# Running the last 64 rows of a 448-row contraction for two output blocks at once, in the two halves of the PE array

## The chip, the cores and the metric

The kernel runs on one core of a Trainium2 chip. The engines are named as in the profiles: PE (TensorE, the matmuls; PEld are its weight loads), ACT (ScalarE), DVE (VectorE), POOL (GpSimdE) and SP, whose queue issues most DMA transfers. PE writes its results to PSUM, a memory which the kernel divides into eight banks; ACT and DVE empty them (an "eviction"). The metric is the device time of one execution in microseconds (us), lower is better. Each version is timed several times beside the kernel before on the same chip.

The kernel before spreads from 334.6 to 340.4 us. Its shorter runs (up to 337 us) have a mean granted clock of 0.969 to 0.980 in the run records and its longer ones (from 338 us) of 0.955 to 0.965; the granted clock is the share of full speed that PE was allowed. A run over 1.5% above the fastest of its kernel counts as slow and is left out, and in some rounds that takes away a few of the longest runs of the kernel before. Differences under 1% are therefore read from intervals and from matmul spacings in the traces, not from single times.

## The reference

Two layers, each a spectral mixing half and a feed-forward half (FFN), over 2048 tokens of width D = 448:

```python
def _B_ref(x, w1, b1, w2, b2):            # the FFN; F = 1792
    h = jnp.einsum("bsd,df->bsf", x, w1) + b1
    r = jnp.where(h > 0, h, 0)
    h = r * r
    return jnp.einsum("bsf,fd->bsd", h, w2) + b2

# _A_ref: irfft2(rfft2(x) * W), computed in the kernel by matmuls with matrices of the Fourier transform
x = x + _A_ref(_layernorm(x), A_w_r, A_w_i)
x = x + _B_ref(_layernorm(x), B_w1, B_b1, B_w2, B_b2)
x = x + _A_ref(_layernorm(x), A_w_r, A_w_i)
x = x + _B_ref(_layernorm(x), B_w1, B_b1, B_w2, B_b2)
```

## The kernel before

The contraction of the first FFN matmul has 448 = 3 x 128 + 64 rows. The kernel before pads the last 64 rows with zero weights to a fourth block of 128. It works in four chunks c of 512 tokens; in each, `h_part` makes 14 blocks of h (128 features x 512 tokens) with 56 matmuls (a "W1 group"), and then four o tiles of 14 matmuls each use them (a "W2 group"). A "slot" below is the time from the start of one matmul to the start of the next.

```python
memset(W1_sb[64:128, 3, :], 0.0)
dma("sp", W1_sb[0:64, 3, :], B_w1[384:448, :])
...
def h_part(c, fb):
    hb = hbuf[c % 2]
    q = _Tile(1)                                  # one PSUM bank
    for blk in range(4):
        mm(q[lambda b: ps[:, b, :]], W1_sb[:, blk, fb * P:(fb + 1) * P], yT[:, 4 * c:4 * c + 4, blk, :],
           blk == 0, blk == 3)
    act(hb[:, fb, :], q[...], ACT.Relu, bias=b1f[:, fb:fb + 1])     # ScalarE empties the bank
    tt(hb[:, fb, :], hb[:, fb, :], hb[:, fb, :], ALU.mult)          # VectorE squares
...
def ffn(last):
    for t in range(0, NT, 2):
        sch.bias = 5500.0 * (NT - t)
        stage_TI(t); stage_AI(t)                  # inverse transforms of two token tiles
        ln_B1(t); ln_B2(t)                        # layer norm, transpose by DMA into yT
    for c in range(4):
        sch.bias = 22000.0 * (4 - c)
        for fb in range(FB):
            h_part(c, fb)
        for t in range(4 * c, 4 * c + 4):
            sch.bias = 5500.0 * (NT - t)
            o_tile(t)
            ...
```

The program's order is not written by hand. Every operation goes to a list scheduler that runs in Python when the kernel is built. It works with modelled costs, and takes next the unit that could start earliest, with ties broken by priority (`prio`, which includes `sch.bias`). All matmuls of one PSUM tile form one unit. The scheduler also picks each tile's PSUM banks, the ones free earliest by its own account:

```python
def pick_banks(n):
    best = None
    for b in range(0, NB, n):
        ok = [bank_user[i] is None or all(op in done for op in bank_user[i].readers) for i in range(b, b + n)]
        if all(ok):
            f = max(bank_free[b:b + n])
            if best is None or f < best[0]:
                best = (f, b)
    return best
...
key = (start, -u.prio, u.seq)
...
for a in (op.gdeps if e != "pe" else ()):         # the account of banks
    if a.eng == "pe" and a.unit.tile is not None:
        for i in range(a.unit.tile.bank, a.unit.tile.bank + a.unit.tile.n):
            bank_free[i] = max(bank_free[i], t + op.lat)
```

So an edit to one tile can change the order of the whole program.

## Time and profile before

| | |
|---|---|
| time | 338.5 us (338.15 to 339.89, 3 runs) |
| span in the profile | 336.8 us |
| PE / DVE / ACT busy | 85% / 61% / 53% |
| one W1 matmul, start to start | 216 ns (duration 379 ns) |

The first lines of the page of the kernel before: span, busy time and share per engine, and further down the shares of the chain that ended last.

```profile
span 336.8 us, 4428 instructions
...
PE 285.0 (85%) x1574; PEld 154.8 (46%) x1574; DVE 205.1 (61%) x499; ACT 178.5 (53%) x293; POOL 56.3 (17%) x81
...
PE 64%; DVE 24%; ACT 5%; issue 2%; POOL 2%; DMA 1%; DVEq 0%; POOLq 0%; ACTq 0%
```

The timeline of PE in the kernel before, second FFN. Columns: start and length in us, engine, source line, operation, output<-inputs, array rows x columns, shape, count; in brackets the idle time just before and what ended it.

```profile
235.60 1.47 PE L454 MATMUL ps<-TI_sb,VT 128*128 128x224 bf16 x8
...
241.90 13.95 PE L454 MATMUL ps<-yT,W_sb 128*128 128x512 bf16 x56 [1.96 <-ACT arena L472]
255.69 10.76 PE L454 MATMUL ps<-W_sb,arena 128*128 128x448 bf16 x56
266.28 12.25 PE L454 MATMUL ps<-yT,W_sb 128*128 128x512 bf16 x56
278.37 10.76 PE L454 MATMUL ps<-W_sb,arena 128*128 128x448 bf16 x56
288.96 10.52 PE L454 MATMUL ps<-yT,W_sb 128*128 128x512 bf16 x48
299.32 0.92 PE L454 MATMUL ps<-XA,FI_sb 128*128 128x448 bf16 x4
300.07 10.76 PE L454 MATMUL ps<-W_sb,arena 128*128 128x448 bf16 x56
310.67 12.25 PE L454 MATMUL ps<-yT,W_sb 128*128 128x512 bf16 x56
322.75 10.76 PE L454 MATMUL ps<-W_sb,arena 128*128 128x448 bf16 x56
```

`yT,W_sb` is the first FFN matmul (W1), `W_sb,arena` the second (W2). From 241.9 us to the end PE never waits. (The W1 group at 241.90 takes 13.95 and not 12.25 us, because seven of its first slots took 427 ns, at a lowered clock.)

### The profile page before, as it was taken

How to read it: one execution, taken by the hardware profiler on the slowest of the kernel's cores; microseconds unless marked ns; L12 is line 12 of the kernel's file. 1: busy time of each engine (PE TensorE's matmuls, PEld its weight loads, DVE VectorE, ACT ScalarE, POOL GpSimd, SP SyncE). 2: the span in 40 equal slices, each digit the busy share in tenths (PEclk: the TensorE clock that was granted, in tenths of full speed). 3: DMA queues.
4: the chain of work that ended last, by engine and by line, in shares of the span. 5: the costliest groups of instructions: out<-in, count | busy, mean ns of one | idle time of the engine just before them, and what ended most of it. 6: DMA issues, size and time to landing. Idle time of an engine off the chain costs nothing.

```text
span 336.8 us, 4428 instructions
## 1 busy us (share of the span) xinstructions
PE 285.0 (85%) x1574; PEld 154.8 (46%) x1574; DVE 205.1 (61%) x499; ACT 178.5 (53%) x293; POOL 56.3 (17%) x81
## 2 busy tenths in 40 slices
PE   0979857857799999899996975774799999999996
PEld 0656534533354454455454652443344445445442
DVE  5705992799867555776455499159973342463432
ACT  2669955655634706645813885555573271451730
POOL 4991000454300000200000000045530000010000
PEclk9999977999999999999999898799789999999999
DMA  7994000033210000010000000002231100002001
GB/s 300 409 371 75 1 2 0 0 69 70 50 34 0 0 2 0 0 34 1 0 2 0 0 2 0 0 0 65 63 79 31 41 0 29 27 0 74 14 14 41
DMA packets 25621, 16.00 MB, mean 48 GB/s; under 512 B 19392, under 2 KB 24000, under 8 KB 25600
## 3 DMA queue, kind: packets, MB, share of 16 engines
q1 hardware_dynamic: 25312, 15.43, 15.0%
q10 hardware_dynamic: 288, 0.30, 0.3%
q8 instruction: 12, 0.20, 0.2%
q14 instruction: 9, 0.07, 0.1%
HBM read 9.70 MB, written 1.84 MB: 34 GB/s over the span
## 4 chain that ended last, share of the span: by engine, by line
PE 64%; DVE 24%; ACT 5%; issue 2%; POOL 2%; DMA 1%; DVEq 0%; POOLq 0%; ACTq 0%
PE ps L454 64%; DVE tmp L476 7%; DVE x_sb L476 4%; DVE st L548 4%; DVE arena L476 3%; DVE tmp L485 2%; ACT arena L472 2%; DVE nmr L559 2%; ACT XA L472 2%; DMA x_sb<-in_A_x_dram 1%; ACT VT L472 1%; POOL Fs L485 1%; DVE mv L549 1%; POOL Ms L485 1%; DVE rstd L556 0%
## 5 line engine op out<-in xcount | busy, mean ns | idle before, releaser
L454 PE MATMUL ps<-yT,W_sb 128*128 128x512 bf16 x448 | 101.7, 387 | 5.6 <-ACT arena L472 5.6
L472 ACT ACTIVATE arena<-ps,b1f 128x512 bf16<-128x512 f32 x112 | 75.3, 685 | 47.0 <-PE ps L454 47.0
L454 PE MATMUL ps<-W_sb,arena 128*128 128x448 bf16 x448 | 86.9, 352 | 0.0
L476 DVE TENSOR_TENSOR arena<-arena 128x512 bf16<-128x512 bf16 x112 | 49.6, 443 | 40.0 <-ACT arena L472 39.9
L454 PEld LDWEIGHTS ps<-yT,W_sb 128*128 128x128 bf16 x448 | 44.2, 99 | 61.2 <-ACT arena L472 8.1
L476 POOL TENSOR_TENSOR arena<-x_sb,b2row 128x896 bf16<-128x896 bf16 x16 | 30.3, 1907 | 215.7 <-DVE x_sb L476 179.5
L454 PEld LDWEIGHTS ps<-W_sb,arena 128*128 128x128 bf16 x448 | 43.8, 98 | 40.1
L472 ACT ACTIVATE XA<-ps 128x512 bf16<-128x512 f32 (+1 forms) x48 | 32.5, 701 | 28.1 <-PE ps L454 27.7
L476 DVE TENSOR_TENSOR x_sb<-ps,arena 128x448 bf16<-128x448 f32 x32 | 19.9, 623 | 37.0 <-PE ps L454 37.0
L548 DVE BATCH_NORM_STATS2 st<-x_sb 128x6 f32<-128x448 bf16 x64 | 38.4, 614 | 3.0 <-DMA x_sb<-in_A_x_dram 2.4
L454 PE MATMUL ps<-H_sb,arena 128*128 128x256 bf16 x128 | 22.9, 330 | 11.3 <-DVE arena L476 9.9
L472 ACT ACTIVATE arena<-ps 128x904 bf16<-128x904 f32 x32 | 28.0, 931 | 5.9 <-PE ps L454 5.6
L472 ACT ACTIVATE rstd<-mv,epst 128x2 f32<-128x2 f32 (+1 forms) x40 | 11.7, 293 | 35.5 <-DVE mv L549 35.4
L476 DVE TENSOR_TENSOR x_sb<-ps,x_sb 128x896 bf16<-128x896 f32 x16 | 16.8, 1071 | 18.6 <-PE ps L454 18.6
L472 ACT ACTIVATE VT<-ps 128x512 bf16<-128x512 f32 (+1 forms) x36 | 18.6, 551 | 13.9 <-PE ps L454 13.6
L454 PEld LDWEIGHTS ps<-H_sb,arena 128*128 128x128 bf16 x128 | 13.5, 115 | 20.5 <-DVE arena L476 14.3
L454 PE MATMUL ps<-XA,FI_sb 128*128 128x448 bf16 x64 | 14.1, 354 | 9.5 <-ACT XA L472 9.5
L485 DVE TENSOR_SCALAR tmp<-x_sb,mv,rstd 128x224 bf16<-128x224 bf16 (+1 forms) x48 | 20.3, 453 | 1.4
L472 ACT ACTIVATE tmp<-x_sb,nmr,rstd 128x448 bf16<-128x448 bf16 x16 | 12.2, 759 | 13.1 <-DVE nmr L559 12.9
L476 DVE TENSOR_TENSOR tmp<-arena 128x904 bf16<-128x904 bf16 (+1 forms) x16 | 8.9, 567 | 16.2 <-ACT arena L472 16.1
L454 PE MATMUL ps<-Fs,x_sb 128*128 128x256 bf16 x32 | 9.8, 324 | 10.0 <-POOL Fs L485 9.1
L454 PE MATMUL ps<-arena,G_sb 128*128 128x452 bf16 (+1 forms) x72 | 15.1, 342 | 3.3 <-ACT arena L472 2.0
(40 smaller groups left out, 208.3 us busy)
## 6 DMA issues: line engine op xcount, KB each, us to landing
x_sb<-in_A_x_dram SPq DMA_DIRECT2D x4, 448.0 KB, 5.3
out_dram<-x_sb SPq DMA_DIRECT2D x16, 112.0 KB, 1.7
W_sb<-in_B_w_dram SPq DMA_DIRECT2D x1, 1568.0 KB, 19.7
W_sb<-in_B_w_dram SPq DMA_DIRECT2D x1, 1344.0 KB, 15.1
yT<-in_A_w_r_dram SPq DMA_DIRECT2D x1, 900.0 KB, 9.1
yT<-in_A_w_i_dram SPq DMA_DIRECT2D x1, 900.0 KB, 10.9
H_sb<-c_H SPq DMA_DIRECT2D x1, 896.0 KB, 12.1
G_sb<-c_G SPq DMA_DIRECT2D x1, 672.0 KB, 7.4
```

Source lines behind the costliest of these rows:

```text
L454: sch.add("pe", lambda e: e.matmul(_res(o), lhsT, rhs, start=start, stop=stop, skip_group_check=skip), [lhsT, rhs], [o], cost=max(_free(rh ...
L472: sch.add("act", lambda e: e.activation(o, _res(i), func, **kw), rd, [o], cost=c)
L476: sch.add(eng, lambda e: e.tensor_tensor(o, _res(a), b, op), [a, b], [o], cost=_free(o) / rate + 65.0)
L485: sch.add(eng, lambda e: e.tensor_scalar(o, i, s1, s2, op0=op0, **kw), rd, [o], cost=_free(o) / (1.4 if eng == "pool" else 1.92) + 65.0)
L548: small(lambda e, t=t: e.bn_stats(st[:, t, 0:6], x_sb[:, t, :]), [x_sb[:, t, :]], [st[:, t, 0:6]], 530.0)
L549: small(lambda e, t=t: e.bn_aggr(mv[:, t, 0:2], st[:, t, 0:6]), [st[:, t, 0:6]], [mv[:, t, 0:2]])
L559: small(lambda e: e.scalar_tensor_tensor(out=n, in0=m, scalar=-1.0, in1=r, op0=ALU.mult, op1=ALU.mult), [m, r], [n])
```

## The change

Two neighbouring blocks of h become one unit with a tile of two banks. Each block's first three matmuls stay. The fourth matmuls, now of 64 rows each, use the lower and the upper half of the array, so that they should stream at the same time. `yT` held the 64 rows twice already.

```diff
-        memset(W1_sb[64:128, 3, :], 0.0)
...
-        dma("sp", W1_sb[0:64, 3, :], B_w1[384:448, :])
+        for i in range(2):
+            dma("sp", W1_sb[64 * i:64 * i + 64, 3, :], B_w1[384:448, :])
...
         def h_part(c, fb):
             hb = hbuf[c % 2]
-            q = _Tile(1)
-            for blk in range(4):
-                mm(q[...], W1_sb[:, blk, fb * P:(fb + 1) * P], yT[:, 4 * c:4 * c + 4, blk, :], blk == 0, blk == 3)
-            act(...); tt(...)
+            q = _Tile(2)
+            yt = yT[:, 4 * c:4 * c + 4]
+            for i in range(2):
+                for blk in range(3):
+                    mm(q[lambda b, i=i: ps[:, b + i, :]], W1_sb[:, blk, (fb + i) * P:(fb + i + 1) * P],
+                       yt[:, :, blk, :], blk == 0, False)
+            for i in range(2):
+                r = slice(64 * i, 64 * i + 64)
+                mm(q[lambda b, i=i: ps[:, b + i, :]], W1_sb[r, 3, (fb + i) * P:(fb + i + 1) * P],
+                   yt[r, :, 3, :], False, True)
+            for i in range(2):
+                act(...); tt(...)                 # as before, per block
...
-                for fb in range(FB):
+                for fb in range(0, FB, 2):
                     h_part(c, fb)
```

The intent is to save one of eight 216 ns slots per pair of blocks.

More of the change, by code (lines that the diff above doesn't have):

```diff
@@ L725, in h_part @@
             hb = hbuf[c % 2]
-            q = _Tile(1)
-            for blk in range(4):
-                mm(q[lambda b: ps[:, b, :]], W1_sb[:, blk, fb * P:(fb + 1) * P], yT[:, 4 * c:4 * c + 4, blk, :],
-                   blk == 0, blk == 3)
-            act(hb[:, fb, :], q[lambda b: ps[:, b, :]], ACT.Relu, bias=b1f[:, fb:fb + 1])
-            tt(hb[:, fb, :], hb[:, fb, :], hb[:, fb, :], ALU.mult)
+            q = _Tile(2)
+            yt = yT[:, 4 * c:4 * c + 4]
+            for i in range(2):
+                for blk in range(3):
+                    mm(q[lambda b, i=i: ps[:, b + i, :]], W1_sb[:, blk, (fb + i) * P:(fb + i + 1) * P], yt[:, :, blk, :],
+                       blk == 0, False)
+            for i in range(2):
+                r = slice(64 * i, 64 * i + 64)
+                mm(q[lambda b, i=i: ps[:, b + i, :]], W1_sb[r, 3, (fb + i) * P:(fb + i + 1) * P], yt[r, :, 3, :],
+                   False, True)
+            for i in range(2):
+                act(hb[:, fb + i, :], q[lambda b, i=i: ps[:, b + i, :]], ACT.Relu, bias=b1f[:, fb + i:fb + i + 1])
+                tt(hb[:, fb + i, :], hb[:, fb + i, :], hb[:, fb + i, :], ALU.mult)
         def o_tile(t):
```

## The prediction

> **What bounds the kernel now.** The page gives a span of 336.8 us with PE busy 85%, DVE 61%, ACT 53%; the chain of waits is 64% PE. In it two long stretches hang on PE almost alone: 90.2 to 179.8 us and 241.9 to 333.5 us, the two FFN halves. The spectral stages are not touched. In the stretches PE's timeline has 56 W1 matmuls (128x512) in 12.25 us and 56 W2 matmuls in 10.76 us without a gap: one W1 matmul costs 216 ns start to start (its listed 379 ns is latency, with a tail of 163 ns that the next one covers). ACT (685 ns per block) and DVE (443 ns) keep up with PE's 864 ns per block. Before 90.2 and 241.9 PE waits for ACT, which stands behind the layer norm on DVE. The granted clock is 1.00, but for the first few us of the second FFN, where it was halved.
>
> **Removed.** A pair of blocks issues eight matmuls before and after, but the last two, of 64 rows each, should stream together in the two halves of the array: one 216 ns slot less per pair, 56 pairs, 12.1 us of PE. The Trainium skill, "TensorE: Matmul & The Clock Gate", Part 3, says that row tiles run concurrently, starting about 4 ns apart; no run shows it yet. 7 pairs (48 W1 matmuls of the first half lie before 90.2, 8 of the second before 241.9) run while PE waits for others anyway; 49 pairs count: 10.6 us at most.
>
> **Added.** One more 224 KB load, early: nothing. PSUM is taken two banks at a time and a pair's evictions come together: under 1 us. The real cost: each pair goes from 128-row to 64-row mode and back, 112 switches. "TensorEngine Tiling (Array Packing)", Key Properties, says that changing the tiling mode drains the TensorE; it gives no time, and the trace before has only 128-row matmuls, so nothing here measures it. Bounds from the trace: weights loaded with nothing ahead delay a matmul by some 10 ns (227 instead of 216 ns at 90.2 us); a full drain would show about the 163 ns tail. A free switch gains 10.6 us, 108 ns per switch nothing, 170 ns loses 6 us. My guess is 70 to 80 ns: 216 - 150 = 66 ns gained per pair, 49 pairs, about 3.3 us.
>
> **Prediction: 335 us**, 8 in 10 between 328 and 344. Faster by over 2%: 0.28; within 2%: 0.60; slower by over 2%: 0.12.
>
> **What would show the steps.** (1) The two 64-row matmuls of a pair start within 10 ns of each other. (2) The first of them starts later than 216 ns after the last full one, or the next full one later than 216 ns after the pair: the excess is the drain, 40 to 110 ns each. (3) A chunk of 56 W1 matmuls takes 11.3 to 12 us instead of 12.25. (4) W2 groups stay at 10.76 us, the spectral stages unchanged; PE stays the chain in both stretches.
>
> **What would make it wrong.** A switch that drains the whole tail, with weight loads that can't be pulled ahead across it (slower); a drain hidden or very short (up to 3% faster); row tiles that don't overlap (no gain and all the cost); a greedy schedule that turns out differently with two-bank tiles, above all in the first chunk, where PE waits for ACT.

## More of the kernel before

Look at the line at 299.32: four small matmuls of the *inverse transform* (the last token pair, t = 14) stand just ahead of the third W2 group. They are the second step of that transform; the first, eight matmuls `TI_sb,VT`, was done at 235.60, ahead of the whole FFN, and ACT carries its result to the second. Their result goes through the layer norm and a DMA transpose into `yT`, which the last W1 group (310.67) needs. All of that happens while PE works off the W2 group at 300.07, so nobody waits for it.

## The result, and the profile after

The changed kernel takes 349.2 us (349.18 to 351.81, 4 runs) against 338.32 us (338.03 to 339.89, 4 runs). Ratios here and below are the mean time of one kernel's fast runs over that of the other's of the same rounds, so they are not quite the ratio of the medians quoted. This one is 1.033 (95% interval 1.027 to 1.039): slower, and outside the predicted range.

The same lines of the page after:

```profile
span 347.4 us, 4466 instructions
...
PE 282.4 (81%) x1574; PEld 142.9 (41%) x1574; DVE 207.1 (60%) x498; ACT 173.2 (50%) x293; POOL 56.5 (16%) x81
...
PE 59%; DVE 27%; ACT 7%; issue 3%; DMA 2%; POOL 2%; POOLq 0%; DVEq 0%; ACTq 0%; SPq 0%
```

PE is *less* busy than before (282.4 against 285.0 us). What was added is time in which PE stands still. The timeline of PE after, second FFN, shows where:

```profile
249.56 5.22 PE L454 MATMUL ps<-yT,W_sb 128*128 128x512 bf16 x24 [1.54 <-ACT arena L472]
254.72 10.77 PE L454 MATMUL ps<-W_sb,arena 128*128 128x448 bf16 x56
265.33 12.12 PE L454 MATMUL ps<-yT,W_sb 128*128 128x512 bf16 x56
277.38 10.77 PE L454 MATMUL ps<-W_sb,arena 128*128 128x448 bf16 x56
287.98 10.40 PE L454 MATMUL ps<-yT,W_sb 128*128 128x512 bf16 x48
298.31 0.94 PE L454 MATMUL ps<-TI_sb,VT 128*128 128x224 bf16 x8
300.55 10.77 PE L454 MATMUL ps<-W_sb,arena 128*128 128x448 bf16 x56 [1.30 <-ACT XA L472]
311.15 0.92 PE L454 MATMUL ps<-XA,FI_sb 128*128 128x448 bf16 x4
319.51 13.82 PE L454 MATMUL ps<-yT,W_sb 128*128 128x512 bf16 x56 [7.44 <-DMA yT<-tmp]
333.26 10.77 PE L454 MATMUL ps<-W_sb,arena 128*128 128x448 bf16 x56
```

The four small inverse-transform matmuls (`XA,FI_sb`) now stand *behind* the third W2 group, at 311.15, and not ahead of it. The place ahead of it has gone to their first step, the eight matmuls `TI_sb,VT` at 298.31. The layer norm and the transpose that need them can't be hidden any more, and PE waits 7.44 us for the DMA into `yT`. The chain after, from there on (start and length in us):

```profile
300.55 11.54 PE ps L454 x60
312.09 0.02 issue
312.11 1.10 DVE x_sb L476
313.21 0.02 issue
313.24 1.15 DVE st L548 x2
...
316.71 2.71 DMA yT<-tmp
319.42 0.09 issue
319.51 24.53 PE ps L454 x112
```

Before, this part of the chain was PE alone, "91.62 PE ps L454 x444". And the wait has an echo: the W1 group behind it takes 13.82 us and not 12.12, because it starts at a lowered clock, after PE stood still. Each engine's busy time in stretches of the changed kernel, with the granted clock (PEclk) after POOL:

```profile
265.00:277.00 12.00, 12.00 (x57) 4.24 (x55) 5.30 (x12) 7.55 (x12) 0.00 (x0) 1.00 0.03 10
315.00:319.50 4.50, 0.00 (x0) 0.02 (x1) 0.64 (x3) 0.76 (x1) 0.45 (x2) 0.65 0.26 58
319.50:325.00 5.50, 5.49 (x18) 1.68 (x19) 0.85 (x2) 1.51 (x3) 0.00 (x0) 0.67 0.00 0
```

The Trainium skill, "TensorE: Matmul & The Clock Gate", Part 1, says that the clock falls to half after an idle window of about 3.4 us; the trace agrees: 427 ns between the matmuls at 320 us, twice the usual 216 ns (the first interval was 380 ns).

From the first W2 group of the second FFN to the end of the last one the kernel before takes 77.8 us (322.75 + 10.76 - 255.69) and the changed one 89.3 us (333.26 + 10.77 - 254.72). The 11.5 us between them are, to 0.1 us: 7.44 us of waiting for the DMA, 1.70 us of slow clock, 1.30 us of waiting for ACT ahead of the third W2 group, and 0.94 us for the eight matmuls `TI_sb,VT`, which the kernel before had run earlier. Up to 254.72 the changed kernel was 1 us ahead; there it was the kernel before whose first W1 group had started at a lowered clock. The first FFN is no slower than before: there its last W2 group ends at 176.91 + 2.81 = 179.72 us, and before at 176.98 + 2.81 = 179.79 us.

And the 64-row matmuls themselves? Start times of single matmuls in one pair, read from the trace of the changed kernel:

```
start us   rows   after the one before
112.127    128    216 ns
112.342    128    215 ns
112.654     64    312 ns     into the 64-row mode: 96 ns more than a slot
112.657     64      3 ns     the second half, together with the first
112.976    128    319 ns     back to 128 rows: 103 ns more than a slot
113.202    128    226 ns     10 ns more
```

The two halves do stream together. The Trainium skill, Part 3 of the same page, says about 4 ns apart; the trace shows 3 ns. But going in costs 96 ns and coming out 103 ns plus 10 or 11 ns on the next matmul, so a pair takes 1,723 ns (112.976 to 114.699) where eight matmuls took 8 x 216 = 1,728 ns. The saved slot is eaten: from the start of a W1 group to the start of the W2 group behind it pass 12.05 us (265.33 to 277.38) and, before, 12.09 us (266.28 to 278.37). The lengths 12.12 and 12.25 in the lists differ by more only because the list lets the last matmul's duration run on into the next group; PE's busy time hides the spacings in the same way.

The trace also shows where the switch waits. Within one mode the weight load of the next matmul starts 1 to 2 ns after the start of the running one (112.128 behind 112.127). At the switch it doesn't: the two loads of 64 rows start at 112.650 and 112.653, 308 ns after the last matmul of 128 rows and 4 ns before the first of 64, and on the way back it is the same (load 112.972, matmul 112.976). All changes of mode in this trace and in that of e4 below have such late loads, nearly all of them 4 or 5 ns ahead of their matmul. So no weights of the new mode are loaded early, and it isn't the length of the load (92 ns) that is waited for.

So the change as such looks neutral, and the 10 us look like an accident of the order. That has to be tested.

### The profile page after: what moved, and what is told of

The parts are those of the page before. It is cut to its first block, busy times and chain, and to the rows that moved or that the text cites. A ratio compares the mean times of both kernels' runs of the same rounds, so it can differ in the third digit from the quotient of the medians.

```text
span 347.4 us, 4466 instructions
## 1 busy us (share of the span) xinstructions
PE 282.4 (81%) x1574; PEld 142.9 (41%) x1574; DVE 207.1 (60%) x498; ACT 173.2 (50%) x293; POOL 56.5 (16%) x81
## 4 chain that ended last, share of the span: by engine, by line
PE 59%; DVE 27%; ACT 7%; issue 3%; DMA 2%; POOL 2%; POOLq 0%; DVEq 0%; ACTq 0%; SPq 0%
PE ps L454 59%; DVE tmp L476 8%; DVE st L548 5%; DVE x_sb L476 4%; ACT arena L472 4%; DVE arena L476 4%; DVE nmr L559 3%; DVE tmp L485 2%; ACT VT L472 1%; DMA x_sb<-in_A_x_dram 1%; ACT XA L472 1%; DVE mv L549 1%; POOL Fs L485 1%; DMA yT<-tmp 1%; POOL Ms L485 1%
## 5 line engine op out<-in xcount | busy, mean ns | idle before, releaser
L454 PE MATMUL ps<-yT,W_sb 128*128 128x512 bf16 x448 | 99.0, 387 | 17.4 <-DMA yT<-tmp 7.4
L472 ACT ACTIVATE arena<-ps,b1f 128x512 bf16<-128x512 f32 x112 | 70.4, 683 | 45.5 <-PE ps L454 45.5
L454 PE MATMUL ps<-W_sb,arena 128*128 128x448 bf16 x448 | 86.9, 353 | 1.3 <-ACT XA L472 1.3
L476 DVE TENSOR_TENSOR arena<-arena 128x512 bf16<-128x512 bf16 x112 | 51.2, 461 | 46.8 <-ACT arena L472 46.7
L454 PEld LDWEIGHTS ps<-yT,W_sb 128*128 128x128 bf16 x448 | 34.4, 97 | 82.5 <-issue 45.4
L454 PEld LDWEIGHTS ps<-W_sb,arena 128*128 128x128 bf16 x448 | 43.3, 98 | 41.4 <-ACT XA L472 1.5
L454 PE MATMUL ps<-H_sb,arena 128*128 128x256 bf16 x128 | 21.7, 316 | 13.0 <-DVE arena L476 11.6
L454 PEld LDWEIGHTS ps<-H_sb,arena 128*128 128x128 bf16 x128 | 12.6, 109 | 22.1 <-DVE arena L476 16.3
L454 PE MATMUL ps<-XA,FI_sb 128*128 128x448 bf16 x64 | 15.4, 382 | 6.7 <-ACT XA L472 6.7
L454 PE MATMUL ps<-Fs,x_sb 128*128 128x256 bf16 x32 | 9.4, 314 | 10.5 <-POOL Fs L485 9.5
L454 PE MATMUL ps<-TI_sb,VT 128*128 128x224 bf16 x128 | 14.1, 260 | 4.6 <-DVE x_sb L476 3.1
L485 DVE TENSOR_SCALAR tmp<-x_sb,mv,rstd 128x224 bf16<-128x224 bf16 (+1 forms) x48 | 16.9, 383 | 1.3
```

Of the source, the lines that this page charges most:

```text
L454: sch.add("pe", lambda e: e.matmul(_res(o), lhsT, rhs, start=start, stop=stop, skip_group_check=skip), [lhsT, rhs], [o], cost=max(_free(rh ...
L472: sch.add("act", lambda e: e.activation(o, _res(i), func, **kw), rd, [o], cost=c)
L476: sch.add(eng, lambda e: e.tensor_tensor(o, _res(a), b, op), [a, b], [o], cost=_free(o) / rate + 65.0)
L485: sch.add(eng, lambda e: e.tensor_scalar(o, i, s1, s2, op0=op0, **kw), rd, [o], cost=_free(o) / (1.4 if eng == "pool" else 1.92) + 65.0)
```

## The experiments

The theory ("order"): the time was lost because the last inverse transform was put behind the third W2 group. The rival ("switches"): it was lost to the changes of mode, directly or by timing. Times are medians; "before" is the kernel before in the same rounds.

### e1: the changed order without any 64-row matmul

```diff
-                r = slice(64 * i, 64 * i + 64)
+                r = slice(0, P)          # 128 rows over the zero padding, as before
```
(with the memset and the single load of before). A listing of the programs shows the order on PE, ACT and POOL to be the same as in the changed kernel; in the two traces it is, and on DVE too, but for the memset.

> The changed kernel's two-bank tiles and, by listing, its very order on PE, ACT and POOL, but all matmuls with 128 rows over a zero-padded block, as before: no mode switch at all. If the lost time comes from the order of the program (the last inverse transform of the second spectral half put behind the third chunk's W2 group), this run stays at 349 us (348 to 351), with the PE idle time of about 7.4 us before the last W1 chunk still there. If it comes from the mode switches, it falls back to 338 us.

Measured: 349.73 us, ratio to before 1.035 (1.027 to 1.044). Two lines of its PE timeline:

```profile
319.78 13.80 PE L454 MATMUL ps<-yT,W_sb 128*128 128x512 bf16 x56 [7.46 <-DMA yT<-tmp]
333.41 10.76 PE L454 MATMUL ps<-W_sb,arena 128*128 128x448 bf16 x56
```

The whole loss is there with not one change of mode. The rival falls. (This kernel still has the tiles of two banks, whose evictions come together; that they are not the cause by themselves is seen in e3.)

### e2: the order of before with the 64-row pairs

The one-bank tiles of before are scheduled as before; then, in the finished list for PE, each pair's first 64-row matmul is moved behind the second block's full ones (all 56 pairs).

```diff
             for blk in range(4):
-                mm(q[...], W1_sb[:, blk, ...], yT[:, 4 * c:4 * c + 4, blk, :], blk == 0, blk == 3)
+                r = slice(64 * (fb % 2), 64 * (fb % 2) + 64) if blk == 3 else slice(0, P)
+                mm(q[...], W1_sb[r, blk, ...], yT[r, 4 * c:4 * c + 4, blk, :], blk == 0, blk == 3)
...
         sch.schedule()
+        pair_halves()                    # pe.insert(j - 1, pe.pop(i))
```

> The other corner: the order and the one-bank tiles of the kernel before, with the 64-row matmuls in pairs (all 56 pairs, the first half moved behind the second block's full matmuls after scheduling). If the order is the cause: 338 us (337 to 339.5), as the switches measured in the changed kernel's trace (96 ns going in, 103 to 106 ns going out) nearly eat the slot of 216 ns saved: 4 ns per pair. If the switches are the cause: 349 us.

Measured: 339.27 us against 338.7, ratio 1.005 (0.998 to 1.012). The last W1 group follows the third W2 group without a wait:

```profile
311.04 12.12 PE L454 MATMUL ps<-yT,W_sb 128*128 128x512 bf16 x56
```

With the old order no gain or loss from the 64-row pairs shows, and the spacings are those of the changed kernel (312, 3 and 318 ns). e1 and e2 are the two missing corners of a square: the order, with the tiles that it belongs to, moves the time, and the 64-row mode doesn't.

### e3 and e3b: one priority

```diff
-                sch.bias = 5500.0 * (NT - t)
+                sch.bias = 5500.0 * (NT - t) + (32000.0 if last and t == NT - 2 else 0.0)   # e3; 20000.0 in e3b
                 stage_TI(t)
```

In e3 no inverse transform is left behind the third W2 group (by the scheduler's list the last pair goes ahead of the FFN, and the pair before it, t = 12, takes the place ahead of that group); in e3b the last one gets ahead of the last of the four o tiles only.

> The changed kernel with one number changed: the last group (t = 14) of the second half's inverse transform gets a higher scheduling priority, so that its last four matmuls and the layer norm after them come ahead of the third chunk's W2 group again. Order theory: the 7.4 us of idle PE and the slow-clock start of the last W1 chunk (1.7 us) go, 338 to 340 us. Switch theory: unchanged at 349 us.

> A half dose of the priority change: in the changed kernel the last inverse transform of the second half moves ahead of only one of the four o tiles behind which it stood (14 W2 matmuls, 2.65 us on PE). Order theory: the idle PE before the last W1 chunk shrinks from 7.4 to about 4.8 us, and the kernel takes 346 to 347 us. If the order were only a bystander: 349 us, and the idle time does not follow the move.

Measured: e3 338.28 us, ratio 1.001 (0.990 to 1.012), repeated as e3r with more rounds below; e3b 345.34 us, ratio 1.023 (1.016 to 1.030). From the PE timelines of e3 (W2 and W1) and, below, of e3b:

```profile
298.18 10.76 PE L454 MATMUL ps<-W_sb,arena 128*128 128x448 bf16 x56
308.77 12.12 PE L454 MATMUL ps<-yT,W_sb 128*128 128x512 bf16 x56
```

```profile
308.04 2.81 PE L454 MATMUL ps<-W_sb,arena 128*128 128x448 bf16 x14
315.85 13.62 PE L454 MATMUL ps<-yT,W_sb 128*128 128x512 bf16 x56 [5.00 <-DMA yT<-tmp]
```

The idle time follows the dose: 7.44, then 5.00 (e3b), then 0 us (e3). As e3 keeps the tiles of two banks and all the switches, neither of them costs the 10 us by itself. One W2 tile (2.65 us start to start) of advance took 2.44 us off the wait. (e3b's time fell by more, some 3.9 us; the wait of 1.30 us ahead of the third W2 group shrank to 0.58 us as well.)

> The changed kernel with only the priority raised, once more, with more rounds and on the same chip as the two kernels that build on it. 337 to 339 us, within 1% of the kernel before.

Measured: 337.12 us against 338.71, ratio 1.002 (0.996 to 1.008).

### e4: each 64-row matmul alone

As e2, without moving the halves together, so there are twice as many switches and nothing streams together.

```diff
         sch.schedule()
-        pair_halves()
```

> The order of before with the 64-row matmul of each block alone at its place: no two stream together, and there are twice as many mode switches. If a switch costs about 100 ns whatever the neighbour is, each block pays about 200 ns more than before (98 blocks on PE's stretches, 112 in all): 358 us (356 to 361). If the gap seen in the changed kernel belongs to starting two tiles at once, and not to changing the mode, it stays at 338 us.

Measured: 360.01 us, ratio 1.065 (1.053 to 1.078). The spacings are 312 ns going in (112 of them) and 319 ns coming out, and a chunk takes 15.08 us instead of 12.25:

```profile
279.67 15.08 PE L454 MATMUL ps<-yT,W_sb 128*128 128x512 bf16 x56
```

So the 96 and 103 ns belong to the change of mode and not to running two halves at once. The Trainium skill, "TensorEngine Tiling (Array Packing)", Key Properties, says that a change of mode drains the TensorE, without a time; here it is about 100 ns each way.

### e5 and e7: fewer switches for the same slots

If the switch is what eats the gain, halves of neighbouring pairs should share one stay in the 64-row mode. In every second pair the halves come first.

```diff
+            front = (fb // 2) % 2        # e5, on the order of before; e7 does the same on e3
+            if front: halves()           # start=True here
             ... six full matmuls ...
+            if not front: halves()
```

> The order of before with the 64-row halves paired, and every second pair has its halves first and not last, so that the halves of two neighbouring pairs stand together: 8 switches per chunk and not 14, for the same slots saved. If each pair of switches costs about 200 ns and nothing else: three of them less per chunk, 0.6 us per chunk on some 7 chunks of PE's stretches: 4.3 us less than the kernel before, 334 to 335 us. If the gap belonged to something else (a 64-row matmul as such), no gain: 338 to 339 us.

> The changed kernel with the priority raised, and in every second pair the two 64-row matmuls first, so that neighbouring pairs share one stay in the 64-row mode. By the earlier traces (a chunk of 56 W1 matmuls in 11.5 instead of 12.1 us, six chunks on PE's stretches, about 0.5 us each): 3 us less than the kernel with the priority alone, 334 to 336 us. No gain if switches hide elsewhere.

Measured: e5 336.43 us against 338.41, ratio 1.000 (0.990 to 1.010), a miss; e7 334.69 us against 338.71, ratio 0.994 (0.988 to 1.001), within what was expected. The chunk does get shorter, 11.60 us in both:

```profile
265.10 11.60 PE L454 MATMUL ps<-yT,W_sb 64*128 64x512 bf16 x56
```

From start to start that is 11.53 us, 0.5 us less per chunk than in the changed kernel. With six chunks on PE's stretches it can bring some 3 us, which these runs can't tell clearly from noise: the interval of e7 just includes no gain.

### e6: all of W1 in the 64-row mode, four blocks at a time

448 = 7 x 64. If all seven halves run in the 64-row mode, a pair takes seven double slots instead of eight, with two switches per chunk. A first layout let the two halves of the array exchange their banks without a wait. The matmuls of the two halves run at the same time, 3 ns apart in the traces above, and nothing ordered their writes to one bank. In e6 four blocks run interleaved, and a wait on PE's own semaphore, placed four slots later, orders the exchange.

```diff
+    parts = [(blk, g) for blk in range(4)] + [(blk, 1 - g) for blk in range(3)]    # g = fb % 2: half of the array
+    # blocks s, t, u, v: slots 0-3 of s,t; 0-3 of u,v; 4-6 of s,t; 4-6 of u,v
```

> Nearly the whole first FFN matmul in the 64-row mode, order of before: the 448 rows are seven halves of 64, so two blocks take seven double slots instead of eight, and four blocks run interleaved so that a bank is never written by both halves of the array in a row (a wait on PE's own semaphore between, long satisfied). Two switches per chunk. If weight loads stay hidden in this mode: 49 slots of 216 ns per chunk and one pair of switches, about 10.9 us instead of 12.25, 9 us less on PE's stretches: 329 us (328 to 332). If weight loads can't be pulled ahead between two 64-row tiles, each slot gets some 10 to 100 ns longer: 333 to 365 us.

Measured: 348.59 us. Two of the four runs, and the profile, fell in the slow state; the fast ones took 346.08 and 345.56 us. A miss: the ratio of the fast runs is 1.024 (1.014 to 1.035). In the profile, which is one of the slow runs, PE waited for ACT again and again (each wait 0.2 to 2.1 us), in the last chunk too:

```profile
333.40 3.56 PE L454 MATMUL ps<-yT,W_sb 64*128 64x512 bf16 x27 [0.18 <-ACT arena L472]
```

I took the evictions, which now come four at a time, for the cause; that was not isolated, and the faulty account of banks found below is a rival that was not tested on this layout.

### e8: the same mode, pipelined by pairs

On e3. The second part of a pair (slots 4 to 6) goes behind the first part of the next pair, so pairs complete evenly; the first chunk of each half is as in e7.

```diff
+    for u in run:                        # neighbouring pairs
+        out.extend(u.ops[:8])            # slots 0-3, two halves each
+        if late is not None:
+            out.extend(late.ops[8:])     # slots 4-6 of the pair before
+        late = u
```

> As that one in the first chunk of each half; in the other three chunks all of the first FFN matmul in the 64-row mode, seven double slots per pair, with the second part of a pair behind the first part of the next, so that pairs complete evenly and a bank changes between the halves of the array with 4 slots of another pair between. If what slowed the run with four blocks at once was the bunched evictions and not the mode itself, PE no longer waits for ACT in these chunks: 98 matmuls in 10.8 us instead of 12.25, six chunks, some 8 us less than the kernel before: 328 to 332 us. If the wait for PE's own semaphore or the banks stall PE again: 335 us or more.

Measured: 344.7 us (one of six runs slow), ratio 1.023 (1.014 to 1.032): again a miss of the hoped-for 328 to 332 us. But its PE timeline is a surprise:

```profile
268.49 10.75 PE L454 MATMUL ps<-yT,W_sb 64*128 64x512 bf16 x98
279.18 10.77 PE L454 MATMUL ps<-W_sb,arena 128*128 128x448 bf16 x56
...
314.73 3.20 PE L454 MATMUL ps<-yT,W_sb 64*128 64x512 bf16 x28 [1.46 <-ACT arena L472]
319.38 1.69 PE L454 MATMUL ps<-yT,W_sb 64*128 64x512 bf16 x14 [1.46 <-ACT arena L472]
...
```

A middle chunk takes 10.75 us instead of 12.25 without one wait. Double slots start 216 ns apart (median of that chunk, none above 227), so the weight loads stay hidden. Of the chunks kept in the mode only the last of each half stalls, four times by 1.46 to 1.48 us. The scheduler's list shows why: in the last chunk of the second half the pairs get only the banks 0-1, 6-7, 0-1, 2-3, 0-1, 2-3, 0-1, while 4-5 stay unused. The account of banks (shown above) marks the banks of *every* PE operation that another engine's operation depends on. When ACT overwrites an h buffer that an old o tile had read, the bank of that o tile counts as just used, though it was emptied long ago.

### e10, e11, e12: the account of banks mended

```diff
-                    if a.eng == "pe" and a.unit.tile is not None:
+                    if a.eng == "pe" and a.unit.tile is not None and op in a.unit.tile.readers:
```

This one line goes into e8 (e10), into the kernel before (e11, as the control) and into the changed kernel (e12).

> The pipelined kernel with its scheduler's account of free banks mended: there, an ACT write to a buffer that an old o tile had read marked that o tile's banks as just used, so that the last chunk's pairs got only two pairs of banks in turn, and PE waited 1.46 us for ACT before each. If that is the cause of the last chunk's stalls, they go (4 or 5 of 1.46 us in each half, 12 to 14 us in all), the last chunk takes 10.8 us like the other two, and the kernel 329 to 332 us. If the stalls come from the 64-row mode or from PE's own semaphore: 342 to 345 us again.

> Control: the kernel before with the same one-line mend of the scheduler and nothing else. Its groups of matmuls have no stalls to lose, but the order changes a little in the spectral halves: within 1% of the kernel before, 335 to 340 us. If it reached 331 us, the gain of the run beside it would be the scheduler's and not the 64-row mode's.

> The changed kernel, untouched but for the one-line mend of the scheduler's account of free banks. By listing, the last inverse transform then stands ahead of the third chunk's W2 group again. If the mistaken account is what put it behind once tiles took two banks: no 7.4 us of idle PE, and, as a pair of switches costs what a pair's saved slot brings, the same time as the kernel before with the same mend: 327 to 330 us. If two-bank tiles or the switches cost something of their own on a sound schedule: 333 to 339 us, as the kernels with the raised priority.

| kernel with the mend | median us (range) | ratio to the kernel before (95%) |
|---|---|---|
| e10: pipelined 64-row mode | 324.05 (320.5 to 325.25) | 0.960 (0.953 to 0.966) |
| e11: kernel before | 328.45 (328.07 to 330.7) | 0.976 (0.970 to 0.982) |
| e12: changed kernel | 330.7 (329.58 to 331.1) | 0.977 (0.973 to 0.981) |

The last two W1 groups of e10, and below those of e11:

```profile
277.78 9.24 PE L454 MATMUL ps<-yT,W_sb 64*128 64x512 bf16 x84
...
298.41 10.75 PE L454 MATMUL ps<-yT,W_sb 64*128 64x512 bf16 x98
```

```profile
278.40 10.52 PE L454 MATMUL ps<-yT,W_sb 128*128 128x512 bf16 x48
...
300.11 12.25 PE L454 MATMUL ps<-yT,W_sb 128*128 128x512 bf16 x56
```

The stalls of e8 are gone, as expected, and e10 is faster than the 329 to 332 us that were expected. The control missed its expectation: the mend alone makes the kernel before 2.4% faster, because its order in front of the FFNs improves as well (the first chunk's W1 group of the first FFN starts at 74.54 us and W2 at 88.35; before, W2 started at 93.71; in the second FFN W2 starts at 245.13, before at 255.69, and that is the whole gain). What the 64-row mode and the pipelining add beyond that is 323.8 / 329.1 = 0.984 by the means of the same rounds (e10 also carries e3's priority and two-bank tiles). That is 5.4 us, less than the 1.41 us of each of six chunks (12.09 and 10.68 us from start to start). Some of the rest is the clock: in the two profiled runs the 70 matmuls behind the first FFN take 11.63 us in e10 and 10.04 in e11, at granted clocks of 0.72 and 0.86 from 174 to 186 us, and the 1.6 us by which e10 led there are gone.

In e12 the order is right again, by itself:

```profile
281.11 10.40 PE L454 MATMUL ps<-yT,W_sb 128*128 128x512 bf16 x48
291.44 0.93 PE L454 MATMUL ps<-XA,FI_sb 128*128 128x448 bf16 x4
292.21 10.76 PE L454 MATMUL ps<-W_sb,arena 128*128 128x448 bf16 x56
302.80 12.12 PE L454 MATMUL ps<-yT,W_sb 128*128 128x512 bf16 x56
```

The time, 330.7 us, lies just above the expected 327 to 330. With the mend in both, the kernels with and without the change have ratios of 0.977 and 0.976 to the kernel before (measured on two chips, intervals overlapping): it is neutral, to about half a per cent. So the bad order took two things together, tiles of two banks and the mistaken account.

The schedulers were run again with every choice printed (the times here are the scheduler's own model). In the kernel before, the first step of the last pair (`stage_TI`, t = 14) gets its banks at 221.2 us, just before the first block of h is ready, at 221.9. In the changed kernel no pair of banks is free for it, by the account, until 222.7. By then the first two blocks of h are ready too (222.0), both could start at once, and h has the higher priority. From there on `stage_TI` loses every tie until the third W1 group is through; its second step then stands behind the four o tiles of the third W2 group. With the mend (e12) it gets its banks at 215.5, ahead of h (217.4).

## Why the prediction was right or wrong

- **What bounds the kernel: right.** PE alone carries both FFN stretches, and a W1 slot is 216 ns.
- **Removed, one slot per pair: right.** The halves start 3 ns apart.
- **Added, two switches per pair: the mechanism was right, the size too small.** The guess was 70 to 80 ns; the traces have 96 ns in and 103 ns out, plus 10 or 11 ns. That is near the break-even of 108 ns that the prediction named. The expected gain of 66 ns per pair (3.3 us in all) is 4 to 5 ns per pair in the trace, some 0.04 us per chunk, so the chunk takes 12.12 us and not the predicted 11.3 to 12.
- **"PSUM is taken two banks at a time and a pair's evictions come together: under 1 us": this step failed.** It is the term that decided. It cost 10.4 us (7.44 waiting, 1.70 slow clock, 1.30 before W2), though at most the last of these has to do with the evictions: the scheduler reacted to two-bank tiles with another order. The prediction did list a greedy schedule that turns out differently as a risk, "above all in the first chunk, where PE waits for ACT". The choice did fall just ahead of that chunk, by the scheduler's printed choices; what was not foreseen is that its cost comes three chunks later, at the last chunk's input, where PE had no other work to fill the wait. The sum gave that risk no term, and the range was too narrow above for it.
- **W2 groups at 10.76 us: right** (10.77). **"PE stays the chain in both stretches": wrong** in the second, where DVE and a DMA broke into it at 312 us.

## What to carry to other kernels

When a scheduler orders the program, list the order before and after an edit, and look for small producers that have slid behind a long group: their cost is the whole latency behind them, not their own microsecond. A packed mode pays only if its stay is long enough for what it costs to go in and out: at about 210 ns per stay here, one saved 216 ns slot was worth nothing, while a chunk kept in the mode (49 double slots for 56) saved 1.4 us. And an experiment that stalls where its twin doesn't is worth a look at the bookkeeping: here one wrong line of accounting was worth more than the change under study.

## What the Trainium skill lacked or had wrong

- "TensorEngine Tiling (Array Packing)", Key Properties, says that a change of tiling mode drains the TensorE, without a time. Here: 96 ns from 128-row to 64-row matmuls, 103 ns back, plus 10 or 11 ns on the matmul after; 312 and 319 ns start to start against 216 ns, the same in pairs and alone (e4). The weights of the new mode are not loaded ahead across the change (load 4 ns before the matmul).
- "TensorE: Matmul & The Clock Gate", Part 3, says in its list of what overlaps that LDWEIGHTS overlaps with in-flight matmuls only when the row groups differ (elsewhere the page does not limit it so). Taken alone this is too narrow: in the kernel before, each 128-row load (98 ns) starts 1 to 2 ns after the start of a matmul in the same rows, and slots stay at 216 ns; in e8 both halves load new weights for every double slot, and these follow each other at 216 ns too.
- The same page, "Back-to-back issue gap", gives about 131 ns per matmul at N = 512 in a sustained stream (elsewhere the page has the figure that the trace shows). Here 440 successive pairs of W1 matmuls in the kernel before have a median of 216 ns and none below 215 ns.
- No page that I used says that running a contraction of an odd number of 64-row halves entirely in the 64-row mode is an option; here it took a chunk from 12.25 to 10.75 us.
